# Block 3's first quarter of H by halves, and the order of sums and activations in Y of blocks 1 to 3

## The chip, the cores and the metric

The kernel runs on one core of one Trainium2 chip. The time is that of the device for one execution, in microseconds (us). Three runs of the kernel before gave 274.15, 274.19 and 273.52 us, so its median is 274.15 us.

The engines have short names in the profile: PE is TensorE (matrix products; PEld is its loading of weights), DVE is VectorE, ACT is ScalarE, POOL is GpSimd and SP is SyncE, which here only issues transfers.

## The reference

Linear attention with phi(x) = elu(x) + 1 over 8 batches of 8 heads, 576 rows and 64 columns, followed by two matrix products with a swish between them:

```python
q_p, k_p = phi(q), phi(k)                       # 8 x 8 x 576 x 64
kv  = einsum('bhsd,bhse->bhde', k_p, v)
z   = sum(k_p, axis=2)
num = einsum('bhsd,bhde->bhse', q_p, kv)
den = einsum('bhsd,bhd->bhs', q_p, z)[..., None] + 1e-06
x   = (num / den), as 4608 x 512
h   = x @ w_in                                  # 512 x 2048
g   = h / (1 + exp(-beta * h))
out = g @ w_out                                 # 2048 x 512
```

## The kernel before, in words

**Blocks and stages.** A block is one batch. Of its 576 rows 512 go through the two big products as a block; the 64 rows left over of all eight batches together make a last block, number 8. After a long start (block 0 and the attention of block 1) a loop runs over b = 1 to 8. Each turn has two stages: H (x times w_in, then swish into g, 16 tiles `ff` of 128 columns of w_in) and Y (g times w_out into the output). Beside these two stages of block b the attention of block b+1 (kv, numerators, transposes of x) runs in H, and phi of block b+2 runs in Y.

**The order is written by hand.** The program is scheduled manually: each engine executes its instructions in the order of the source. A step of the attention is hung onto a step of H or Y with `at(sh, n, f)` or `at(sy, n, f)`, and `run(side, n)` issues it there. So the numbers in the loop at the end of the file (lines 1031 to 1074) are the schedule.

**H in two forms.** `h_phase` makes all 16 tiles plainly: four matmuls of 512 columns into one PSUM bank, then one activation (`silu`). `h_fast` makes tiles 0 to 3 by halves instead: seven products of half size (`h_products`, four matmuls of 256 columns each, 28 in all against 16 of 512) of sums of w_in (`h_w_sums`, once) and of sums of x (`h_x_sums`, once per block: four subtractions on DVE into `h_xs`, which is the memory of `xs_sb`). Six DVE sums (`part0` to `part3`) put the products together, and `out` activates the results. Between the products stand plain tiles, so that DVE has time. Before the change blocks 1 to 3 use `h_phase`, blocks 4 to 8 `h_fast`; blocks 7 and 8 make two quarters by halves.

**Y** (`y_fast`) uses halves throughout: seven products of 16 matmuls of 256 columns, in the order pa, pd, pa, pc, pb, pd, pb, on four banks. DVE makes `gs` for it (`g_diff`, `g_sums`), u2 and u3 (lines 987 and 988) and the four quarters of the result. The second product into pb can start only when the sum at line 997 has read the first; the second into pd only when line 988 has read pd.

**PSUM.** Pool `hps` has four single banks that go round among the plain tiles, the first half product, two banks of the numerators, and Y. Pool `wps` has two pairs that go round among kv, the numerators (`numer_all`, two pairs) and the half products (`hc`, `hz`).

**Queues.** SyncE issues the transposes of phi of q (`q_trans_dma`, tile qTd) and of x (`trans` in `numer_all`, tile xT) and the stores of the output, in program order. GpSimd issues the loads: `next_loads(n)` first copies one element of qTd (`gate`), so that nothing is loaded for the next block before the transposes have landed, then issues v, q and k of block n+1, and casts v (`v_copy`). `tail_copy` saves the 64 rows left over, also on GpSimd.

Of the kernel before, what the change touches and what calls it, by code (L numbers as in the profile page):

```python
# [11 lines left out]
ACTF = mybir.ActivationFunctionType  # L12
# [4 lines left out]
def kernel(  # L17
# [39 lines left out]
    def banks(name, shape=None, dt=F32):  # L57
        return wps.tile(shape or [P, 2, 512], dt, tag="w", name=name)
# [95 lines left out]
    def table(func):  # L154
        nc.scalar.activation(act0, warm[:, 0:1], func)  # L155
# [57 lines left out]
    def kv_both(b):  # L213

        t = banks("kvp")
        for pr in range(2):
            for j in range(J):  # L220
                for il in range(2):
                    for a in range(2):
                        nc.tensor.matmul(  # L223
                            t[half(il), a, pr * EA : (pr + 1) * EA],
                            st[b, "k"][half(a), pr, j, il * D : (il + 1) * D],
                            vaug[b % 2][half(a), pr, j, il, 0:EA],
                            start=(j == 0), stop=(j == J - 1), skip_group_check=True,
                        )
        tv = t[:, :, 0 : 2 * EA].rearrange("p a (r e) -> p a r e", r=2)
        if b > 1:  # L230
            nc.vector.tensor_copy(kv_q[b % 2], tv)
            return
        st[b, "kv"] = kv_bd.rearrange("p a r h e -> p a r (h e)")
        for il in range(2):
            nc.vector.tensor_copy(kv_bd[half(il), :, :, il], tv[half(il)])
# [83 lines left out]
    def numer_all(b):  # L319

        h = [bank("nps"), bank("nps")]
        w = [banks("nps") for _ in range(2)]
        for v in (*range(7, 14), *range(7), *range(14, 18)):
            t, a = v // 4, v % 2
            for il in range(2):
                ps = h[il] if v // 7 == 1 else w[v // 14][:, il]  # L330
                for n in range(2):
                    pr, j = (v % 4 // 2, 2 * t + n) if v < 16 else (n, J - 1)
                    nc.tensor.matmul(
                        ps[half(n), v % 7 * EA : (v % 7 + 1) * EA],
                        st[b, "qTd"][half(il), a, pr * J + j, :],
                        kv_q[b % 2][half(il), a, pr, :],
                        start=True, stop=True, skip_group_check=True,
                    )

        def evac(ps, ils, v0, v1):  # L340

            m, i, u = len(range(*ils.indices(2))), v0 % 7, v1 - v0
            pv = ps[:, :, i * EA : (i + u) * EA].rearrange("p i (u e) -> p i u e", e=EA)
            den = work.tile([P, 2, 7], F32, tag="den", name="den")[:, :m, :u]
            rden = work.tile([P, 2, 7], F32, tag="rden", name="rden")[:, :m, :u]
            nc.vector.tensor_scalar(den, pv[:, :, :, D], 1e-6, None, ALU.add)
            nc.vector.reciprocal(rden, den)
            nc.vector.tensor_mul(  # L348
                xs_sb[:, ils, v0 * D : v1 * D].rearrange("p i (u d) -> p i u d", d=D),
                pv[:, :, :, 0:D], rden[:, :, :, None].to_broadcast([P, m, u, D]),  # L350
            )

        def trans(v0, v1):
            for il in range(2):
                nc.sync.dma_start_transpose(
                    out=xT[b % 2][:, il, v0 // 2 : v1 // 2],
                    in_=xs_sb[:, il, v0 * D : v1 * D],
                )

        for il in range(2):  # L360
            evac(h[il][:, None], slice(il, il + 1), 7, 14)
        evac(w[0], slice(0, 2), 0, 7)
        trans(0, 8)
        evac(w[1], slice(0, 2), 14, 18)
        trans(8, 18)
# [349 lines left out]
    def run(side, n):  # L715
        for f in side.get(n, ()):
            f()

    def at(side, n, *fs):
        side.setdefault(n, []).extend(fs)  # L720
# [69 lines left out]
            return xT_tail[:, :, 4 * t : 4 * t + 4, r]  # L790
        return xT[b % 2][:, :, 4 * t + r : 4 * t + 4 : 2]

    def h_x_sums(b, ks=range(4)):

        t = [h_xs[:, k] for k in range(4)]
        x = lambda r, t: h_x_plain(b, r, t)

        def like(a, c):
            return a.rearrange("p i (t n) -> p i t n", n=c.shape[-1])

        for k in ks:
            u, w = (
                (x(0, 1), x(0, 0)), (x(1, 1), t[0]), (x(1, 1), x(0, 1)), (x(1, 0), t[1])
            )[k]
            nc.vector.tensor_sub(like(t[k], u), u, like(w, u) if k % 2 else w)

    def h_products(b, fq):
# [55 lines left out]
    def h_fast(b, x, side):  # L863
        hps_of = {}

        def plain(ff):
            hps_of[ff] = bank("h_ps")
            h_mm(x, ff, hps_of[ff])

        def act(*ffs):  # L870
            for ff in ffs:
                silu(b, ff, hps_of[ff])

        def dual(*ffs):
            for ff in ffs:
                plain(ff)
                act(ff)

        if b < B - 1:
            dual(4)  # L880
            run(side, 0)
        p0, p1, p2, p3, out = h_products(b, 0)
        p0()

        dual(*((5,) if b < B - 1 else (4,)))
        p1()
        dual(*((6,) if b < B - 1 else (5,)))
        p2()
        dual(*((7,) if b < B - 1 else (6,)))
        p3()  # L890
        out(0)
        if b < B - 1:
            g_diff(b, slice(4, 8))
            dual(8, 9)
            out(1)
            run(side, 9)
            for ff in range(10, FC):
                dual(ff)
                if ff == 10:
                    g_diff(b, slice(0, 4))  # L900
                if ff in (11, 15):
                    g_sums(b, ff - 11, ff - 7)
            return
        run(side, 0)
        dual(7)
        out(1)
        p0, p1, p2, p3, out = h_products(b, 2)
        p0()
        dual(12)
        p1()  # L910
        dual(13)
        p2()
        g_diff(b, slice(0, 4))
        dual(14)
        p3()
        out(1, [0])
        g_diff(b, slice(4, 8))
        dual(15)
        out(1, [1])
        out(0)  # L920
        g_sums(b, 4, 8)
        g_sums(b, 0, 4)
# [108 lines left out]
    for b in range(1, B + 1):  # L1031
        n, m = b + 1, b + 2
        sh, sy = {}, {}
        if 2 <= b < 4 or b == B - 1:
            at(sh, 0, lambda: tail_copy(b))
        if n < B:
            at(sh, 0, lambda: next_loads(n))
            if b >= 4:
                at(sh, 0, lambda: tail_copy(b))
            at(sh, {1: 9, 2: 2}.get(b, 1 if b == 3 else 0), lambda: kv_both(n))  # L1040
            at(sh, {1: 11, 2: 5}.get(b, 4 if b == 3 else 9), lambda: numer_all(n))
        if b == 1:
            at(sh, 4, lambda: w_sum(2))
            at(sh, 9, lambda: w_sum(1))
            at(sy, 0, lambda: w_sum(3))
        if m < B:
            at(sy, 0, lambda: phi_tile(m, "q"), lambda: phi_tile(m, "k"))
            if b == 1:

                for pr in range(2):  # L1050
                    at(sy, 0, lambda pr=pr: v_copy(nc.scalar, m, pr))
                for pr in range(2):
                    at(sy, 0, lambda pr=pr: phi_exp(m, "q", pr, xin(m, "q", pr)))
                    at(sy, 3 + pr, lambda pr=pr: phi_relu(m, "q", pr, xin(m, "q", pr)))
                    at(sy, 3 + pr, lambda pr=pr: phi_min(m, "q", pr))
                at(sy, 4, lambda: q_trans_dma(m))
                at(sy, 5, lambda: phi_part(m, "k", 0))
                at(sy, 6, lambda: phi_part(m, "k", 1), lambda: table(ACTF.Silu))
            else:
                at(sy, 0, lambda: phi_part(m, "q", 0))  # L1060
                at(sy, 1, lambda: phi_part(m, "q", 1))
                at(sy, 1, lambda: q_trans_dma(m))
                at(sy, 3 if b < 4 else 4, lambda: phi_part(m, "k", 0))
                at(sy, 4, lambda: phi_part(m, "k", 1), lambda: table(ACTF.Silu))
        if b == 3:
            at(sh, 2, lambda: h_w_sums(0))
        if b == B - 2:
            at(sy, 4, lambda: h_w_sums(2))
        if 3 <= b < B:

            for i, step in enumerate((1, 6) if b < B - 2 else (0, 0)):
                at(sy, step, lambda i=i, n=n: h_x_sums(n, range(2 * i, 2 * i + 2)))
        (h_phase if b < 4 else h_fast)(b, xT[b % 2] if b < B else xT_tail, sh)
        y_fast(b, sy)


# [28 lines left out]
```

## Time and profile before

| | us |
|---|---|
| median of the three runs | 274.15 |
| the profiled execution's own time | 274.97 |
| its span, first to last instruction | 273.2 |
| PE busy | 265.4 (97%) |
| DVE busy | 204.1 (75%) |
| ACT busy | 168.8 (62%) |
| POOL busy | 43.6 (16%) |

The page gives for each engine the time in which it was busy. The "chain that ended last" is followed back from the last instruction, at each step to what released it; read in order of time it shows which engine carried the end. In that chain and in a timeline a line holds the start in us, the duration in us, the engine, the line of the source, the instruction's operands by their names in the program, and how many were merged (x16). In brackets stands how long the engine was idle before, and who released it. In the list of waits a line holds who waited, for whom, the total in us, how often, and the longest. PE's granted clock was 0.994 of full speed on average over the span.

### The profile page before, as it was taken

The numbers are of one execution on the slowest core, as the hardware profiler recorded it, in microseconds if no ns is written. First come the engines' busy times: TensorE is split into PE (matmuls) and PEld (weight loads), VectorE is DVE, ScalarE is ACT, GpSimd is POOL, SyncE is SP. The second block draws the span as 40 slices with busy tenths as digits, with TensorE's granted clock in tenths as the row PEclk, the third lists the DMA queues.
The fourth block names the chain that finished last, engine by engine and source line by source line (L and its number), as shares of the span: only waits on it lengthen the run. The fifth ranks groups of instructions, "written<-read, shape, count | busy, mean of one in ns | idle before, by whom it ended". The sixth has DMA issues, their size and how long they took to land.

```text
span 273.2 us, 6742 instructions
## 1 busy us (share of the span) xinstructions
PE 265.4 (97%) x2845; PEld 181.3 (66%) x2845; DVE 204.1 (75%) x392; ACT 168.8 (62%) x237; POOL 43.6 (16%) x64
## 2 busy tenths in 40 slices
PE   7899999999999999999999999999999999999994
PEld 2585455445865487548864886488657866886793
DVE  4871775899895778668868987898788767856862
ACT  3828896976777785588548854886473038405810
POOL 5922002034014020330033003300001000000000
PEclk9979999999999999999999999999999999999999
DMA  6999999656998996998589777995504050024013
GB/s 229 254 206 350 244 396 240 202 104 213 224 115 174 280 165 114 255 241 96 86 231 251 108 91 195 265 132 86 156 2 86 2 154 4 0 43 113 0 41 115
DMA packets 48958, 42.78 MB, mean 157 GB/s; under 512 B 30352, under 2 KB 40736, under 8 KB 48928
## 3 DMA queue, kind: packets, MB, share of 16 engines
q0 software_dynamic: 13040, 23.40, 36.8%
q1 hardware_dynamic: 35568, 18.75, 34.5%
q8 instruction: 22, 0.36, 0.5%
q10 hardware_dynamic: 320, 0.20, 0.3%
q14 instruction: 8, 0.07, 0.1%
HBM read 36.71 MB, written 9.44 MB: 169 GB/s over the span
## 4 chain that ended last, share of the span: by engine, by line
PE 79%; DVE 10%; DMA 6%; ACT 2%; issue 1%; SPq 0%; DVEq 0%
PE h_ps L402 30%; PE yd L964 9%; PE ya L964 9%; PE yb L964 8%; PE hc L820 4%; PE yc L964 4%; PE y_ps L417 4%; DMA xT<-xs_sb 4%; PE hz L820 3%; DMA stage<-in_q_dram 2%; PE kvp L223 2%; ACT g L856 1%; PE yb L936 1%; DVE r L169 1%; DVE phi_k L175 1%; DVE xs_sb L348 1%
## 5 line engine op out<-in xcount | busy, mean ns | idle before, releaser
L410 ACT ACTIVATE g<-h_ps,beta_c 128x512 bf16<-128x512 f32 x116 | 77.0, 688 | 58.7 <-PE h_ps L402 58.7
L402 PE MATMUL h_ps<-xT,w_in 128*128 128x512 bf16 (+1 forms) x480 | 100.0, 358 | 0.7 <-ACT g L410 0.5
L402 PEld LDWEIGHTS <-w_in 128*128 128x128 bf16 x512 | 46.9, 98 | 44.8 <-issue 0.9
L964 PEld LDWEIGHTS <-stage 128*128 128x128 bf16 x480 | 46.9, 98 | 5.8 <-issue 0.3
L964 PEld LDWEIGHTS <-g 128*128 128x128 bf16 x384 | 37.5, 98 | 6.0
L964 PE MATMUL ya<-w_out,g 128*128 128x256 bf16 x256 | 30.6, 273 | 0.0
L241 POOL CAST vaug<-vf 128x1152 bf16<-128x1152 f32 x11 | 12.8, 1190 | 43.0 <-DMA vf<-in_v_dram 15.4
L348 DVE TENSOR_TENSOR xs_sb<-nps,rden 128x448 bf16<-128x448 f32 (+2 forms) x24 | 18.2, 758 | 0.8
L162 ACT ACTIVATE e<-xk 128x1152 bf16<-128x1152 bf16 (+1 forms) x15 | 16.7, 1160 | 3.1 <-DMA xk<-in_k_dram 3.1
L162 ACT ACTIVATE e<-xq 128x1152 bf16<-128x1152 bf16 x14 | 15.6, 1159 | 2.4 <-DMA xq<-in_q_dram 2.0
L728 DVE TENSOR_TENSOR stage<-g 128x1024 bf16<-128x1024 bf16 x16 | 12.8, 798 | 5.6 <-ACT g L410 5.6
L155 ACT ACT_TABLE_LOAD x12 | 15.4, 1283 | 0.2
L964 PE MATMUL yd<-ws,stage 128*128 128x256 bf16 x128 | 15.3, 273 | 0.0
L964 PE MATMUL yc<-ws,stage 128*128 128x256 bf16 x128 | 15.3, 273 | 0.0
L964 PE MATMUL yd<-ws,g 128*128 128x256 bf16 x128 | 15.3, 273 | 0.0
L417 PE MATMUL y_ps<-w_out,g 128*128 128x512 bf16 x64 | 15.1, 379 | 0.0
L175 DVE TENSOR_TENSOR phi_q<-e,r 128x1152 bf16<-128x1152 bf16 x16 | 12.1, 758 | 3.2 <-ACT e L162 2.0
L175 DVE TENSOR_TENSOR phi_k<-e,r 128x1152 bf16<-128x1152 bf16 x16 | 12.8, 802 | 1.4
L964 PE MATMUL yb<-ws,stage 128*128 128x256 bf16 x112 | 13.4, 273 | 0.0
L964 PE MATMUL yb<-w_out,stage 128*128 128x256 bf16 x112 | 13.4, 272 | 0.0
L856 ACT ACTIVATE g<-hc,beta_c 128x512 bf16<-128x512 f32 x14 | 8.8, 682 | 6.8 <-DVE hc L849 6.8
L724 DVE TENSOR_TENSOR stage<-g 128x1024 bf16<-128x1024 bf16 x16 | 10.9, 682 | 1.9 <-ACT g L410 1.9
(135 smaller groups left out, 345.0 us busy)
## 6 DMA issues: line engine op xcount, KB each, us to landing
vf<-in_v_dram POOLq DMA_DIRECT2D x7, 1152.0 KB, 9.5
out_dram<-y SPq DMA_DIRECT2D x29, 256.0 KB, 4.3
xq<-in_q_dram POOLq DMA_DIRECT2D x7, 576.0 KB, 12.4
xk<-in_k_dram POOLq DMA_DIRECT2D x7, 576.0 KB, 15.1
w_in<-in_moe_w_in_dram POOLq DMA_DIRECT2D x4, 512.0 KB, 11.7
g<-in_moe_w_out_dram POOLq DMA_DIRECT2D x2, 1024.0 KB, 17.5
stage<-in_moe_w_out_dram POOLq DMA_DIRECT2D x2, 1024.0 KB, 21.4
stage<-in_q_dram SPq DMA_DIRECT2D x2, 576.0 KB, 4.6
```

Of the source, the lines that this page charges most:

```text
L155: nc.scalar.activation(act0, warm[:, 0:1], func)
L162: nc.scalar.activation(e, x, ACTF.Exp)
L175: nc.vector.tensor_tensor(st[b, a][:, pr].rearrange("p j (h d) -> p j h d", h=2), st[b, a, pr, "e"].rearrange("p h j d -> p j h d"), st[b, ...
L241: eng.tensor_copy(dst, src)
L348: nc.vector.tensor_mul(xs_sb[:, ils, v0 * D : v1 * D].rearrange("p i (u d) -> p i u d", d=D), pv[:, :, :, 0:D], rden[:, :, :, None].to_bro ...
L402: nc.tensor.matmul(hp[:, c0:c1].rearrange("p (t n) -> p t n", n=n), w_in_sb[ff // 4][:, kc, (ff % 4) * P : (ff % 4 + 1) * P], xm, start=(k ...
L410: nc.scalar.activation(g_sb[b % 2][:, ff, :], hp, ACTF.Silu, scale=beta_c[:, ff : ff + 1])
L417: nc.tensor.matmul(yp[:, c0:c1], g_sb[b % 2][:, ff, t * P : (t + 1) * P], w_out_sb[i][:, c, c0:c1], start=(ff == 0), stop=(ff == FC - 1), ...
L728: nc.vector.tensor_add(gs[0][:, c], g[:, c, HM:512], g[:, c2, HM:512])
L820: nc.tensor.matmul(o, lhs[:, i, a * P : (a + 1) * P], m, start=(first and a == 0 and i == 0), stop=True, skip_group_check=True,)
L856: nc.scalar.activation(g_sb[b % 2][:, ff].rearrange("p (t n) -> p t n", t=2), src, ACTF.Silu, scale=beta_c[:, ff : ff + 1],)
L964: nc.tensor.matmul(ps[:, p * HM : (p + 1) * HM], lhs(c, p), rhs(c), start=(first and p == 0 and c == 0), stop=True, skip_group_check=True,)
```

## The change

Five things change, and the step numbers that follow from them.

1. `h_phase` runs for blocks 1 and 2 only; block 3 now uses `h_fast`. `h_w_sums(0)` moves from H of block 3 (step 2) to H of block 2 (step 9).
2. In `h_fast` of blocks 3 to 6 the plain tile 5 comes before the first half product, and the plain tiles between the products are one number higher. The numerators move from step 9 to step 10. In block 3 kv moves from step 1 to 0 and the numerators from step 4 to 10; in block 2 kv from 2 to 3 and the numerators from 5 to 6.
3. The four sums of x stand together behind Y (step 6 of Y of blocks 2 to 5). Before, two stood at step 1 of Y and two at step 6, for blocks 3 to 5. In Y of blocks 6 and 7 they stay at step 0.
4. In `numer_all` the two pairs of banks change places.
5. In Y of block 1 the operations of phi are spread anew over the steps: maximum of q's second half at step 5, minima of q at 4 and 5, transposes of q at 5 instead of 4, and k's parts at 5 and 6. In Y of blocks 2 and 3 the first half of phi of k moves from step 3 to 4. On GpSimd the tail copy of block 3 moves behind the loads.

```diff
-        w = [banks("nps") for _ in range(2)]
+        w = [banks("nps") for _ in range(2)][::-1]
...
-    def h_x_sums(b, ks=range(4)):
+    def h_x_sums(b):
...
+        n = 6 if b < B - 1 else 4
         if b < B - 1:
             dual(4)
             run(side, 0)
+            dual(5)
         p0, p1, p2, p3, out = h_products(b, 0)
         p0()
-        dual(*((5,) if b < B - 1 else (4,)))
+        dual(n)
         p1()
-        dual(*((6,) if b < B - 1 else (5,)))
+        dual(n + 1)
         p2()
-        dual(*((7,) if b < B - 1 else (6,)))
+        dual(n + 2)
         p3()
         out(0)
         if b < B - 1:
             g_diff(b, slice(4, 8))
-            dual(8, 9)
+            dual(9, 10)
             out(1)
-            run(side, 9)
-            for ff in range(10, FC):
+            run(side, 10)
+            for ff in range(11, FC):
                 dual(ff)
-                if ff == 10:
+                if ff == 11:
                     g_diff(b, slice(0, 4))
                 if ff in (11, 15):
                     g_sums(b, ff - 11, ff - 7)
...
-        if 2 <= b < 4 or b == B - 1:
+        if b == 2 or b == B - 1:
             at(sh, 0, lambda: tail_copy(b))
         if n < B:
             at(sh, 0, lambda: next_loads(n))
-            if b >= 4:
+            if b > 2:
                 at(sh, 0, lambda: tail_copy(b))
-            at(sh, {1: 9, 2: 2}.get(b, 1 if b == 3 else 0), lambda: kv_both(n))
-            at(sh, {1: 11, 2: 5}.get(b, 4 if b == 3 else 9), lambda: numer_all(n))
+            at(sh, {1: 9, 2: 3}.get(b, 0), lambda: kv_both(n))
+            at(sh, {1: 11, 2: 6}.get(b, 10), lambda: numer_all(n))
...
-                    at(sy, 3 + pr, lambda pr=pr: phi_relu(m, "q", pr, xin(m, "q", pr)))
-                    at(sy, 3 + pr, lambda pr=pr: phi_min(m, "q", pr))
-                at(sy, 4, lambda: q_trans_dma(m))
-                at(sy, 5, lambda: phi_part(m, "k", 0))
-                at(sy, 6, lambda: phi_part(m, "k", 1), lambda: table(ACTF.Silu))
+                    at(sy, 3 + 2 * pr, lambda pr=pr: phi_relu(m, "q", pr, xin(m, "q", pr)))
+                    at(sy, 4 + pr, lambda pr=pr: phi_min(m, "q", pr))
+                at(sy, 5, lambda: q_trans_dma(m))
+                for pr in range(2):
+                    at(sy, 5, lambda pr=pr: phi_exp(m, "k", pr, xin(m, "k", pr)))
+                    at(sy, 5 + pr, lambda pr=pr: phi_relu(m, "k", pr, xin(m, "k", pr)))
+                    at(sy, 6, lambda pr=pr: phi_min(m, "k", pr))
+                at(sy, 6, lambda: table(ACTF.Silu))
...
-                at(sy, 3 if b < 4 else 4, lambda: phi_part(m, "k", 0))
+                at(sy, 4, lambda: phi_part(m, "k", 0))
...
-        if b == 3:
-            at(sh, 2, lambda: h_w_sums(0))
+        if b == 2:
+            at(sh, 9, lambda: h_w_sums(0))
...
-        if 3 <= b < B:
-            for i, step in enumerate((1, 6) if b < B - 2 else (0, 0)):
-                at(sy, step, lambda i=i, n=n: h_x_sums(n, range(2 * i, 2 * i + 2)))
-        (h_phase if b < 4 else h_fast)(b, xT[b % 2] if b < B else xT_tail, sh)
+        if 2 <= b < B:
+            at(sy, 6 if b < B - 2 else 0, lambda: h_x_sums(n))
+        (h_phase if b < 3 else h_fast)(b, xT[b % 2] if b < B else xT_tail, sh)
```

More of the change, by code (lines that the diff above doesn't have):

```diff
@@ L799, in like @@
             return a.rearrange("p i (t n) -> p i t n", n=c.shape[-1])
[L801 to L804, printed above, removed]
+        for k, (u, w) in enumerate((
+            (x(0, 1), x(0, 0)), (x(1, 1), t[0]), (x(1, 1), x(0, 1)), (x(1, 0), t[1])
+        )):
             nc.vector.tensor_sub(like(t[k], u), u, like(w, u) if k % 2 else w)
```

## The prediction

> **What bounds the kernel now.** I read the page's busy shares first, then the chain that ended last, then the timelines of VectorE, GpSimd and SyncE around the places that the diff touches.
>
> ```profile
> PE 265.4 (97%) x2845; PEld 181.3 (66%) x2845; DVE 204.1 (75%) x392; ACT 168.8 (62%) x237; POOL 43.6 (16%) x64
> PE 79%; DVE 10%; DMA 6%; ACT 2%; issue 1%; SPq 0%; DVEq 0%
> ```
>
> TensorE is busy 97% of the span, and from block 2 on the chain is almost only PE. So a change is worth the PE time it takes out plus the PE waits it removes or makes. Nothing else counts until PE waits for it. The chain in order of time (start, duration, what), from the second product of Y of block 2 that ends late to the middle of H of block 4:
>
> ```profile
> 104.55 1.75 PE yd L964 x16
> 106.30 1.89 PE yb L964 x16
> 108.19 1.73 PE h_ps L402 x8
> 109.91 0.86 PE kvp L223 x72
> 110.77 2.70 PE h_ps L402 x12
> 113.47 0.76 PE nps L333 x72
> 114.23 9.60 PE h_ps L402 x44
> 123.83 1.75 PE ya L964 x16
> ...
> 136.06 0.86 PE h_ps L402 x4
> 136.93 0.74 PE kvp L223 x72
> ...
> 143.45 0.71 DVE hc L849
> 144.19 1.26 ACT g L856 x2
> 145.45 0.59 ACT g L410
> 146.08 5.34 PE h_ps L402 x24
> 151.42 1.75 PE ya L964 x16
> ```
>
> Differences of these starts give the stages: H of block 3, all plain, takes 123.83 - 108.19 = 15.64 us; H of block 4, with a quarter by halves, 151.42 - 136.06 = 15.36 (blocks 5 and 6: 15.38 and 15.37). Y of block 2 takes 12.37, Y of block 3 and later 12.23. The four lines before 146.08 are the price of the halves: the last sum of the products (L849), two activations of them and one of a plain tile must end before PE gets its next bank. PE's starts put that wait at 0.25 us (from the numerators' last matmul to the next 0.37 us; 0.125 in blocks 2 and 3).
>
> VectorE in Y of block 2, and the cast on GpSimd with the VectorE sum beside it in H of block 3:
>
> ```profile
> 103.57 0.69 DVE L988 TENSOR_TENSOR u<-yd,u 128x512 f32<-128x512 f32 x1
> 104.17 0.59 DVE L169 TENSOR_SCALAR r<-xk 128x1152 bf16<-128x1152 bf16 x1
> 104.87 0.76 DVE L175 TENSOR_TENSOR phi_k<-e,r 128x1152 bf16<-128x1152 bf16 x1
> 105.55 0.68 DVE L997 TENSOR_TENSOR y<-yb,u 128x512 f32<-128x512 f32 x1
> ```
> ```profile
> 119.96 2.24 POOL L241 CAST vaug<-vf 128x1152 bf16<-128x1152 f32 x2 [8.42 <-DMA vf<-in_v_dram]
> ```
> ```profile
> 121.14 1.60 DVE L728 TENSOR_TENSOR stage<-g 128x1024 bf16<-128x1024 bf16 x1 [2.04 <-ACT g L410]
> ```
>
> L997 frees the bank of the last product of Y. It stands behind phi of k, ends at 106.23, and that product, due at 106.14, starts 0.146 us late: the 0.14 by which Y of block 2 is long. And a bf16 sum that takes 0.69 us elsewhere took 1.60 while GpSimd cast.
>
> **Part 1: block 3 by halves.** Removed: 16 matmuls of 512 columns, 4 of which are 0.86 us in the chain, 3.46 us. Added: 28 of 256 columns, 4 of which are 0.435 (0.44, and 0.87 for 8), 3.05 us. Gain 0.41. The bank wait comes along: order and banks behind the last product are those of blocks 4 to 6, only the tile numbers are one higher, so +0.25. The kv product took 0.86 in block 3 and 0.74 elsewhere, by one pause of 0.105 in the middle that no other block has; I take it as gone, -0.11. Sum -0.27, which is 15.64 against the 15.36 to 15.38 of the blocks that do this already. If the pause stays, -0.16.
>
> The Trainium skill speaks against such halving ("TensorE: Matmul & The Clock Gate", Back-to-back issue gap): in a real stream it gives some 131 ns for a matmul of 512 columns and some 81 for 128. By that, as an estimate, 16 x 131 = 2.1 us would give way to at least 28 x 81 = 2.3, a loss of 0.2 or more. The chain's 216 and 109 ns per matmul decide against it.
>
> VectorE gains work in block 3: six sums of 0.69 (4.1 us) in H, four x sums of 0.42 behind Y of block 2 (1.6), and h_w_sums moves to step 9 of block 2 (1.5). Cover: h_w_sums falls between g_diff and g_sums, where VectorE idles 1.28 us at 91.8 to 93.1; the numerators' evacuation, a tile later, eats 0.86 of that, so g_sums(0:4) ends some 1 us later, while the next sum waits for ACT until 96.58 anyway. The x sums run 109.0 to 110.6, the kv copy to 111.0; the first product's result is there at about 111.0. Without that cover each would hold the products by its own length.
>
> **Part 2: numerators a tile later, blocks 3 to 6.** PE does the same work in another order: 0. In VectorE everything from the evacuation on moves 0.86 us. Covers, from block 4's rows: the second sum L729 ends 154.05 + 0.86 = 154.9, needed half a product into yc (156.66 in the chain); g_diff(0:4) ends 150.7 + 0.86 = 151.5, needed at 153.2; phi of q ends 0.86 later, but the two x sums that stood there (0.87 us) are gone, and VectorE idled 0.42 before u2. The four transposes of x go out 0.86 later, with nothing else in SyncE's queue then; in block 6 they land at 210.8 + 0.9, the four x sums end at 213.4, and u2 starts at 213.7. So 0, with 0.3 us left at the narrowest place. In block 3 the numerators move by six tiles: its four transposes start at about 122.0 instead of 117.5, and with the 8.4 to 10 us that they took under load they land by 132, before H of block 4 at 135.5. In block 2 kv and numerators move one tile: x lands at 103.9 + 0.9, needed at 107.9: 0. The x sums all behind Y: four end 1.6 us after L1008, before the copy of the first product, which itself comes 0.86 later: 0.
>
> **Part 3: order of two banks.** Numerators 0 to 6 take the pair that the second product frees, 14 to 17 that of the first. The burst of 72 took 0.76 with and without halves, so it did not wait: 0.
>
> **Part 4: Y of blocks 1 and 2.** Block 2: L997 starts when its product ends, 104.6 instead of 105.55; the 0.146 goes. Next on the path is kv of block 4, now at step 0: phi of k ends at 107.8, PE gets there at 108.8. Block 1: L997 stands before phi's minimum, so the same wait (0.16 before the last product, 77.6) goes, but H of block 2 waits for x's transposes (landing about 79.8 and 80.3) whatever Y does:
>
> ```profile
> PEld L402 <- DMA xT<-xs_sb: 0.3, 1, 0.3
> ```
>
> So 0 from block 1. The step to watch is the transpose of q for block 3, moved to step 5. SyncE before, and the gate on GpSimd that starts all loads of the next block:
>
> ```profile
> 79.20 3.54 SPq L273 DMA_TRANSPOSE qTd<-phi_q  x2
> ```
> ```profile
> 85.56 0.53 POOL L1025 COPY gate<-qTd 128x1 bf16<-128x1 bf16 x1 [4.42 <-DMA qTd<-phi_q]
> ```
>
> It now queues behind phi of q, whose minimum ends at 79.7 (79.05 before), and behind two stores of y2 (0.6 each, from 78.5): issue about 79.85, 0.65 later. How much longer the stores ahead of it in the same queue hold it no row shows. Call the whole delay d: at least 0.65, at most, by the far row of x's transposes under load (10.7 us to landing against 4.2 for q's), 7. I take 0.95: no loads run at that time (the last landed at 78.7), and the stores themselves took 1.2 longer behind transposes than later ones alone (4.4 against 3.2), of which I give a quarter. What d meets: numerators of block 3, at PE 87.1, bear d = 1.6. The loads for block 4 move by d, so does the cast, which holds a sum of block 2 until it ends (98.15 + d); phi of q then ends at 102.1 + d and u2, due at 102.84, slips by d - 0.81; the next product into its bank has 0.07 to spare. So Y of block 2 loses d - 0.88: 0.07 for my d.
>
> In block 3 the cast ends at 122.2 + d, near the end of the evacuation (122.8), so g_diff slips by some 0.2, with over 1 us left before Y needs it. The Trainium skill ("SBUF — State Buffer", Who interferes with whom) says that an operation with two SBUF inputs and a GpSimd read exclude each other for a whole instruction, which would fit the 1.60; if a full cast of 1.15 hit there, it would still be under that slack. On GpSimd, block 3's tail copy now stands behind the loads and casts; only the last stage reads it: 0.
>
> **Sum.** -0.27 - 0.146 + 0.07 = -0.35 us. On the profiled execution's own time (274.97, a span of 273.2 and 1.8 around it) that is 274.62; it ran 0.82 over the median of the runs, so on the median of 274.15 it is 273.8. A measurement here tells 0.3%, 0.82 us, from no change.
>
> **Rivals.** (a) *Late q, slower.* If the transposes start only when the stores have landed (stores took 3.6 to 4.4 us, so 83 instead of about 80.5), d is about 3.1 and Y of block 2 with H before it loses 3.1 - 0.88 = 2.2: 274.15 - 0.42 + 2.2 = 275.9. It decides from d = 2.1 on (0.42 + 0.82 + 0.88). For it: x's transposes under load take 10 us. Against: stores and transposes overlap at 82.85, where a store issued before the transposes had landed was only 1.2 late.
> (b) *Nothing comes of it.* The kv pause returns (0.11), d is 1.2 (0.32): -0.42 + 0.11 + 0.32 is no change, 274.1. For it: every term is a tenth of a microsecond. Against: three blocks run the same H at 15.36 to 15.38.
> (c) *Clearly faster.* The bank wait of 0.25 goes in all four blocks with the new order, 0.98 in all: 272.8. For it: numerators take two of four banks, and their place moves. Against: the tiles around them move along.
>
> **How the numbers follow.** Forecast 0.58, (b) 0.20, (a) 0.14, (c) 0.08. The forecast's own range is 273.4 to 274.2. Forecast and (b) are within 0.3%, save some 0.08 that the runs' own spread (273.52 to 274.19) puts over a bound, half on each side: faster 0.12, same 0.70, slower 0.18. The range reaches up to d = 2, 274.15 - 0.42 + 1.12, about 274.9, and down to 273.1, a third of the way to (c); two thirds of (a) and (c) stay out, 0.15.
>
> **What would show it.** H of block 3 at 15.36 to 15.4 with the chain through L849 and L856 as in block 4; Y of block 2 at 12.23 to 12.3; H and Y of blocks 4 to 6 unchanged within 0.05. The gate of block 2 at 86.2 to 86.6. Wrong if Y of block 2 is over 13, if the numerators of block 2 wait for qTd, if a yc or yd product waits for VectorE in blocks 3 to 6, or if H of block 2 starts later than 80.1.

## The result

The changed kernel takes 275.28 us, the median of 21 runs (274.50 to 276.99); the kernel before takes 274.15 us in 21 runs of the same session (273.43 to 274.85). The ratio is 1.0047, with a 95% interval of 1.0033 to 1.0061: slower by about 1.1 to 1.3 us, where 273.8 us was forecast. It is rival (a), in which the transposes of q come late.

The page of the changed kernel hides it well. PE's share of the span falls by one point. In the summary of the chain PE falls from 79% to 66% and DMA rises from 6% to 17%, but 8 points of the 17 are a load of v that the chain now meets in the long start (19.03 to 40.64 us), which the change leaves alone:

```profile
PE 263.3 (96%) x2852; PEld 181.7 (66%) x2857; DVE 208.4 (76%) x402; ACT 167.8 (61%) x237; POOL 43.9 (16%) x64
PE 66%; DMA 17%; DVE 10%; ACT 3%; issue 1%; SPq 1%; POOL 0%; DVEq 0%; POOLq 0%
```

The chain in order of time (start, duration, what) shows the place. These are its lines from the end of x's transposes in Y of block 1 to the half products of block 3:

```profile
70.62 8.81 DMA xT<-xs_sb
...
79.97 1.67 SPq L273
...
81.68 6.08 DMA qTd<-phi_q
...
87.80 0.83 PE nps L333 x72
88.63 7.88 PE h_ps L402 x36
96.50 1.75 PE ya L965 x16
...
108.73 0.86 PE h_ps L402 x4
109.59 0.78 PE kvp L223 x72
110.38 0.97 PE h_ps L402 x4
111.35 0.44 PE hz L819 x4
...
117.03 0.71 DVE hc L848
...
117.76 1.27 ACT g L855 x2
119.03 0.59 ACT g L410
...
119.66 4.48 PE h_ps L402 x20
124.14 1.75 PE ya L965 x16
```

The numerators of block 3 (nps at 87.80) hang on the transposes of q, qTd, which are now on the path. Before, the path ran through PE here without a break:

```profile
83.62 2.69 PE h_ps L402 x12
86.32 0.76 PE nps L333 x72
```

PE's timeline of the changed kernel gives the wait in brackets, and SyncE's shows what stands ahead of the transposes now:

```profile
87.80 0.83 PE L333 MATMUL nps<-kv_q,qTd 64*64 64x65 bf16 x72 [1.48 <-DMA qTd<-phi_q]
```
```profile
78.04 1.31 SPq L1005 DMA_DIRECT2D out_dram<-y  x2
79.52 4.08 SPq L273 DMA_TRANSPOSE qTd<-phi_q  x2
83.71 2.04 SPq L1011 DMA_DIRECT2D out_dram<-y  x2
```

The prediction had named this wait as a sign of being wrong. PE's starts give the stages from H of block 2 on, each from its first matmul to that of the next (the differences are taken before rounding). Spans can't be compared directly: H of block 1 began at 50.6 to 53.3 us in the profiles of this study, after a start that the change leaves alone, and the profiled execution of the kernel before (274.97 us) was one of its longer runs.

| stage | before, us | changed, us | difference |
|---|---|---|---|
| H of block 2 | 15.73 | 17.28 | +1.55 |
| Y of block 2 | 12.37 | 12.23 | -0.14 |
| H of block 3 | 15.64 | 15.41 | -0.24 |
| H of blocks 4, 5, 6 | 15.36, 15.38, 15.38 | 15.40, 15.39, 15.37 | +0.05 in all |
| from H of block 2 to the last matmul | 189.25 | 190.45 | +1.20 |

The sum of the stages, 1.20 us, is close to the difference of the medians, 1.13. So everything that the change was worth (-0.38) is there, and one wait of 1.55 us is paid on top: by PE's starts, 1.64 us of pause before the numerators against 0.09 before.

### The profile page after: what moved, and what is told of

Same layout as the page of the kernel before. It is cut to its first block, busy times and chain, and to the rows that moved or that the text cites. A ratio compares the mean times of both kernels' runs of the same rounds, so it can differ in the third digit from the quotient of the medians.

```text
span 273.5 us, 6774 instructions
## 1 busy us (share of the span) xinstructions
PE 263.3 (96%) x2852; PEld 181.7 (66%) x2857; DVE 208.4 (76%) x402; ACT 167.8 (61%) x237; POOL 43.9 (16%) x64
## 4 chain that ended last, share of the span: by engine, by line
PE 66%; DMA 17%; DVE 10%; ACT 3%; issue 1%; SPq 1%; POOL 0%; DVEq 0%; POOLq 0%
PE h_ps L402 21%; DMA vf<-in_v_dram 10%; PE ya L965 9%; PE yd L965 9%; PE yb L965 8%; PE hc L819 5%; PE yc L965 4%; PE hz L819 4%; DMA xT<-xs_sb 3%; DMA qTd<-phi_q 2%; ACT g L855 2%; PE kvp L223 1%; DMA stage<-in_q_dram 1%; PE yb L937 1%; DVE xs_sb L348 1%
## 5 line engine op out<-in xcount | busy, mean ns | idle before, releaser
L410 ACT ACTIVATE g<-h_ps,beta_c 128x512 bf16<-128x512 f32 x112 | 73.9, 690 | 60.3 <-PE h_ps L402 60.3
L402 PE MATMUL h_ps<-xT,w_in 128*128 128x512 bf16 (+1 forms) x464 | 97.7, 357 | 0.9 <-ACT g L410 0.7
L402 PEld LDWEIGHTS <-w_in 128*128 128x128 bf16 x496 | 45.1, 98 | 41.8 <-issue 1.1
L855 ACT ACTIVATE g<-hc,beta_c 128x512 bf16<-128x512 f32 x16 | 10.1, 683 | 8.1 <-DVE hc L848 8.1
L175 DVE TENSOR_TENSOR phi_k<-e,r 128x1152 bf16<-128x1152 bf16 x16 | 12.8, 803 | 1.3
L175 DVE TENSOR_TENSOR phi_q<-e,r 128x1152 bf16<-128x1152 bf16 x16 | 12.1, 758 | 1.9 <-ACT e L162 0.8
L724 DVE TENSOR_TENSOR stage<-g 128x1024 bf16<-128x1024 bf16 x16 | 10.9, 682 | 2.0 <-ACT g L410 2.0
L819 PEld LDWEIGHTS <-w_in 128*128 128x128 bf16 x96 | 9.4, 98 | 4.5
```

The source lines that it names most:

```text
L175: nc.vector.tensor_tensor(st[b, a][:, pr].rearrange("p j (h d) -> p j h d", h=2), st[b, a, pr, "e"].rearrange("p h j d -> p j h d"), st[b, ...
L402: nc.tensor.matmul(hp[:, c0:c1].rearrange("p (t n) -> p t n", n=n), w_in_sb[ff // 4][:, kc, (ff % 4) * P : (ff % 4 + 1) * P], xm, start=(k ...
L410: nc.scalar.activation(g_sb[b % 2][:, ff, :], hp, ACTF.Silu, scale=beta_c[:, ff : ff + 1])
L724: nc.vector.tensor_sub(gs[2][:, c], g[:, c, 0:HM], g[:, c, HM:512])
L819: nc.tensor.matmul(o, lhs[:, i, a * P : (a + 1) * P], m, start=(first and a == 0 and i == 0), stop=True, skip_group_check=True,)
L855: nc.scalar.activation(g_sb[b % 2][:, ff].rearrange("p (t n) -> p t n", t=2), src, ACTF.Silu, scale=beta_c[:, ff : ff + 1],)
```

## The experiments

Times are medians; each run's ratio is to runs of the kernel before on the same chip. "Run 3" is the changed program of experiment 3. Unless said otherwise an edit is to the changed kernel. "Landing" of the transposes is that of the second one, and "the minimum of phi of q" is the last operation of phi (L175), after which the transposes can start.

**1. Stores of y2 behind the transposes.** Only the place of the two stores moves.

```diff
+        if b == 1:
+            run(side, 5)
         for i in range(2) if b < B else ():
             nc.sync.dma_start(out=rows(b, slice(4 + i, 4 + i + 3, 2)), in_=y2[half(i)])
-        run(side, 5)
+        if b != 1:
+            run(side, 5)
```

> The changed kernel with one thing moved: in Y of block 1 the two stores of y2 are issued behind the two transposes of q (and behind phi's operations of that step) instead of ahead of them. VectorE's order stays that of the change. Theory (the stores ahead in SyncE's queue hold the transposes up on the DMA side by some 2 us): the second transpose lands about 2 us earlier against the start of H of block 2, at about +6.6 us, the numerators at +7.2 no longer wait 1.55 us, and the time falls from 275.28 to about 273.7. Rival 1 (the later minimum of phi of q alone makes them late): at least 1 us of the wait stays, time 274.8 to 275.3. Rival 2 (the loss lies in block 3 by halves or later): no change, 275.3.

Measured: 274.16 us, ratio 1.0009 (0.9991 to 1.0027). The wait at the numerators is gone (H of block 2: 15.52). The gate on GpSimd, which starts as soon as the second transpose has landed, stands at 86.02, 6.9 us after the start of H of block 2; in the changed kernel it stood at 87.87, 8.8 after it. But the time stops some 0.45 short of the 273.7 that was expected, and Y of block 2 lost about that much: it took 12.62 instead of 12.23. Its PE line names the sum u3 (L989), which frees the bank of yd:

```profile
103.77 1.47 PE L965 MATMUL yd<-ws,g 128*128 128x256 bf16 x12 [0.23 <-DVE u L989]
```

VectorE before it, in the same run: two sums of g held to 1.5 us (0.69 elsewhere), while GpSimd cast v (95.64 to 98.81), and then phi of q waiting for its exponential, for which ScalarE waited 1.68 us on the load of q.

```profile
96.29 1.52 DVE L729 TENSOR_TENSOR stage<-stage,g 128x1024 bf16<-128x1024 bf16 x1
97.84 1.51 DVE L730 TENSOR_TENSOR stage<-g,stage 128x1024 bf16<-128x1024 bf16 x1
99.28 0.45 DVE L169 TENSOR_SCALAR r<-xq 128x1152 bf16<-128x1152 bf16 x1
100.39 0.76 DVE L175 TENSOR_TENSOR phi_q<-e,r 128x1152 bf16<-128x1152 bf16 x1 [0.67 <-ACT e L162]
```

Against the start of H of block 2 the transposes landed 1.26 us later than before (6.78 against 5.52). The prediction's formula for this price, d - 0.88, gives 0.38; measured 0.39. So close a match is in part luck: in the profile of run 9, whose edit does not touch this stage, Y of block 2 took 12.52 instead of 12.37.

**2. The same stores from GpSimd's queue.**

```diff
-            nc.sync.dma_start(out=rows(b, slice(4 + i, 4 + i + 3, 2)), in_=y2[half(i)])
+            (nc.gpsimd if b == 1 else nc.sync).dma_start(
+                out=rows(b, slice(4 + i, 4 + i + 3, 2)), in_=y2[half(i)]
+            )
```

> The changed kernel, the two stores of y2 in Y of block 1 at the same place of the program but issued from GpSimd's queue instead of SyncE's. It tells whether the same queue is what holds the transposes, or any store in flight with them. Same queue: the numerators' wait of 1.55 us goes, 273.7. Stores in flight on the shared DMA engines: 0.5 to 1.5 us of it stay, 274.2 to 275.3. Rival 2 (block 3): 275.3.

Measured: 275.44 us, ratio 1.0049 (1.0035 to 1.0063). The wait stays at nearly its full size (1.38 us in PE's brackets against 1.48), though SyncE's queue has nothing ahead of the transposes and starts to issue them 0.15 us after the minimum of phi of q:

```profile
79.02 1.25 POOL L1005 DMA_DIRECT2D out_dram<-y  x2 [14.41 <-DVE y L1001]
...
88.08 0.19 POOL L1028 COPY gate<-qTd 128x1 bf16<-128x1 bf16 x1 [7.29 <-DMA qTd<-phi_q]
```
```profile
80.10 4.51 SPq L273 DMA_TRANSPOSE qTd<-phi_q  x2
```

So it is not the order in one queue. Stores that are in flight when the transposes start hold them up, from either of the two queues. The Trainium skill ("DMA: Bandwidth & Descriptors", Issuing engines are not separate DMA queues) states what fits this: transfers of all issuing engines end up on the same 16 DMA engines and interleave, and issuing from another engine saves only the sequencer's time. The run agrees: the stores' packets from GpSimd's queue run until 83.4 us, those of the transposes beside them from 81.7 on, and the wait is about as long from either queue.

**3. Y of block 1 as before.** The steps of phi in Y of block 1 are put back; the rest of the change stays.

> The changed kernel with the steps of phi in Y of block 1 as they were before; all else as changed. Theory and rival 1 both expect the numerators' wait in block 2 to go and the time to be 275.28 - 1.55 = 273.7; the wait of 0.16 us in Y of block 1 comes back, hidden by the wait for the transposes of x at the start of H of block 2. Rival 2 (block 3 by halves or the later stages lose): about 275.3, still slower than before.

Measured: 273.75 us, ratio 0.9986 (0.9973 to 1.0000), as expected. The numerators don't wait, Y of block 2 takes 12.23, H of block 3 15.40. This is the change without the part that lost: faster by 0.3 to 0.4 us, as the sum forecast, though the interval just reaches no change.

**4. Y of block 1 alone.** The kernel before, with only the new steps of phi in Y of block 1.

> The kernel before with the new steps of phi in Y of block 1 alone. Theory: here the numerators of block 3 stand one tile earlier in H of block 2, so they wait 1.55 + 0.86 = 2.4 us for the transposes of q, and the time is about 274.15 + 2.4 = 276.5; at least 276 if the landing is a little earlier. Rival 2: 274.1, no change.

Measured: 275.62 us, ratio 1.0063 (1.0039 to 1.0087). This part alone makes the kernel slower by 1.6 us. The expected 276.5 (at least 276) did not come. The wait was smaller than the 2.4 expected: in the profile, which is of the fastest run, 1.3, since the landing came 7.4 us after the minimum of phi of q, against 8.5 in the changed kernel. The six runs took 274.58 to 277.12 us; that the holding differs from run to run would explain this spread, but only one of them has a profile.

**5. No stores of y2 in block 1.**

```diff
-        for i in range(2) if b < B else ():
+        for i in range(2) if 1 < b < B else ():
```

> The changed kernel with the two stores of y2 in block 1 left out (a quarter of the output of one block is not written); VectorE's and PE's order as changed. It parts the two causes of the late transposes. Theory: the stores in flight hold them by 2 us, so the second lands 6.3 us after the minimum of phi of q instead of 8.5, some 6.5 us after the start of H of block 2, the numerators at +7.2 do not wait, and the time is 275.28 - 1.55 + 0.1 = 273.8. Rival (the later minimum is enough): a wait of 1 us or more stays, 274.8 or more.

This kernel leaves a quarter of one block's output unwritten. Measured: 273.97 us, ratio 0.9985 (0.9963 to 1.0007). The minimum of phi of q is as late as in the changed kernel (0.3 and 0.2 us after the start of H of block 2), the numerators don't wait, Y of block 2 takes 12.23. With runs 1 and 2 this parts the causes. The time from the end of that minimum to the landing of the second transpose was

| kernel | stores of y2 | us |
|---|---|---|
| before; run 3 | behind the transposes | 6.4; 6.2 |
| run 1 | behind the transposes | 6.4 |
| run 5 | none | 6.2 |
| changed | ahead, SyncE | 8.5 |
| run 2 | ahead, GpSimd | 8.0 |
| run 4 | ahead, SyncE | 7.4 |
| run 6 | ahead, SyncE | 8.4 |

Stores ahead cost 1.0 to 2.1 us against the kernel before. The later minimum, by itself, costs another 1.0 against the start of H of block 2 (0.87 ahead of it before, 0.17 after it in the changed kernel), which the numerators' later step just bears.

**6. Numerators of block 3 two tiles later** (step 8 instead of 6 in H of block 2).

> The changed kernel with the numerators of block 3 two tiles later in H of block 2 (step 8). The transposes of q stay late, but PE comes to the numerators at +8.9 us, after their landing at about +8.7. Theory (the loss is the wait at the numerators; the loads for block 4, started by the same landing, cost little): the wait goes, Y of block 2 takes 12.2 to 12.5, time 273.8 to 274.1. Rival (what is late at the numerators is paid again through the loads): Y of block 2 takes 13 or more, 274.7 or more.

Measured: 274.72 us, ratio 1.0019 (0.9999 to 1.0039). This is nearer to the rival: the wait at the numerators goes, but Y of block 2 takes 12.91. About half of the loss is paid elsewhere: from H of block 2 on the profile is 0.86 us longer than run 3's, that of the changed kernel 1.68. The casts now fall on two sums of g, which stand later as well, and u3 comes late for yd:

```profile
96.06 1.59 DVE L729 TENSOR_TENSOR stage<-stage,g 128x1024 bf16<-128x1024 bf16 x1
97.69 1.52 DVE L730 TENSOR_TENSOR stage<-g,stage 128x1024 bf16<-128x1024 bf16 x1
```
```profile
95.97 2.70 POOL L241 CAST vaug<-vf 128x1152 bf16<-128x1152 f32 x2 [4.51 <-PE h_ps L402]
```
```profile
105.09 1.14 PE L965 MATMUL yd<-ws,g 128*128 128x256 bf16 x9 [0.53 <-DVE u L989]
```

Taking the wait away where it shows is not the same as taking the lateness away.

**7. Block 3 plain again**, on the kernel of run 3: `h_phase` for blocks 1 to 3, kv at step 1 and numerators at step 4 in block 3.

> The changed kernel with Y of block 1 as before, and block 3 plain again (kv at step 1 and numerators at step 4 as before); the new steps of blocks 4 to 6, of block 2 and of Y of blocks 2 and 3 stay. It takes the halves' share out of the gain of 0.31 to 0.40 us. Theory: H of block 3 takes 15.6 instead of 15.40, Y of block 2 stays at 12.23, time 273.75 + 0.24 = 274.0. Rival (the halves in block 3 gain nothing in the time, all comes from Y of block 2): 273.75.

Measured: 273.74 us, ratio 0.9987 (0.9977 to 0.9996), against 0.9986 with the halves. That is the rival's time; the times don't tell the halves' share. The profile has H of block 3 at 15.52 plain against 15.40 by halves, 0.12 us; the 15.64 of the kernel before held the pause of 0.105 in kv, which two profiles of the plain block lack (this run and run 9) and two others have (run 4 and run 11).

**8. The last sum of the half products first**, on the kernel of run 3, blocks 3 to 6.

```diff
-            product(z, w(1, 1), t[3], False)
+            if b >= B - 1:
+                product(z, w(1, 1), t[3], False)
             product(cw[:, 0], w(0, 1), h_x_plain(b, 1, 0), False)
             product(cw[:, 1], s[3], h_x_plain(b, 1, 1), False)
+            if b < B - 1:
+                product(z, w(1, 1), t[3], False)
+                nc.vector.tensor_add(cw[:, 1], cw[:, 1], h_u[0])
             nc.vector.tensor_add(c2[:, 0], z, h_u[0])
-            nc.vector.tensor_add(cw[:, 1], cw[:, 1], h_u[0])
+            if b >= B - 1:
+                nc.vector.tensor_add(cw[:, 1], cw[:, 1], h_u[0])
```

> The changed kernel with Y of block 1 as before (273.75), and in the last part of the half products of blocks 3 to 6 another order: the two products into the pair hc first, the one into hz last, and the sum that finishes hc ahead of the other. Nothing is added. Theory (PE's wait of 0.25 us per block behind the numerators is the chain last sum, two activations, one plain activation): the sum starts one product, 0.44 us, earlier, which is more than 0.25, so the wait goes in blocks 3 to 6 and H takes 15.15 there instead of 15.40; time 273.75 - 0.98 = 272.8. Rival (the wait is for the bank behind the numerators' own evacuation or for a late plain tile): H stays at 15.40, time 273.7.

Measured: 272.85 us, ratio 0.9963 (0.9951 to 0.9976), the best of the study, with an interval clear of no change. The chain goes through PE alone here, also behind the numerators:

```profile
115.48 0.44 PE hz L819 x4
115.91 1.73 PE h_ps L402 x8
117.64 0.76 PE nps L333 x72
118.40 4.42 PE h_ps L402 x20
```

H of blocks 3 to 6 takes 15.24, 15.24, 15.21 and 15.22. So the bank wait of 0.25 is gone in each, but 0.08 of it comes back: the first product into hc now starts 0.08 late, behind the sum that still reads that pair. The gain against run 3 is 4 x 0.16 = 0.64, not 0.98; the ratios, 0.9986 and 0.9963, say the same. That the time hit the expected 272.8 is luck: run 3 was timed on another chip, where the kernel before took 274.06 us and not 273.96.

**9. That order alone, on the kernel before** (blocks 4 to 6).

> The kernel before with that order of the last part alone (blocks 4 to 6). Theory: three waits of 0.25 us go, 274.15 - 0.74 = 273.4, H of blocks 4 to 6 at 15.11 to 15.13 instead of 15.36 to 15.38. Rival: 274.1. It also measures this order by itself, without block 3 by halves.

Measured: 273.47 us, ratio 0.9991 (0.9982 to 0.9999), a gain of some 0.25 us by the ratio where 0.74 was expected. H of blocks 4 and 6 takes 15.20 and 15.23, of block 5 15.42: there the sum that reads hc ran late and the product waited 0.29 for it. The gain is there in two of the three blocks.

**10. Both orders:** run 8, and in Y of block 1 the first sum of Y ahead of phi's minima, with transposes and stores in the order of before (`phi_min` of q at step 4 for both halves).

> As the first kernel here, and in Y of block 1 the first sum into the output's second half moved ahead of phi's two minima of q, while the second minimum and the transposes stay ahead of the next sum and of the stores. So the bank wait of 0.16 us in Y of block 1 goes without making the transposes of q later: their second landing stays within 0.3 us of that of the first kernel here. Theory: 272.8 - 0.16 = 272.6, unless x's transposes take the wait's place at the start of H of block 2 (then 272.8). Rival (any new order in Y of block 1 makes the transposes late): the numerators of block 2 wait again, 273.5 or more.

Measured: 272.94 us, ratio 0.9960 (0.9948 to 0.9973), the same as run 8. The transposes land in time, but x's transposes take the place of the bank wait at the start of H of block 2, as the second branch of the expectation has it. Sums ahead of phi do no harm as long as the transposes stay ahead of the stores, and in block 1 they bring nothing.

**11. The new step of phi of k in Y of blocks 2 and 3 alone**, on the kernel before.

> The kernel before with one thing of the change: in Y of blocks 2 and 3 the first half of phi of k at step 4 instead of 3. Theory: Y of block 2 takes 12.23 instead of 12.37 and nothing else moves, 274.15 - 0.14 = 274.0. Rival: the wait moves to kv of block 4 in H of block 3, which then takes 15.66 or more, and the time stays at 274.1.

Measured: 274.19 us, ratio 0.9993 (0.9973 to 1.0014). Y of block 2 takes 12.23 as expected, and H of block 3 stays at 15.63. The time can't tell 0.14 us.

**12. The two pairs of banks in their old order**, on the kernel of run 3.

> The changed kernel with Y of block 1 as before, and the two pairs of banks of the numerators in their old order. Theory: the exchange of pairs was worth nothing, since the burst of 72 never waited; in blocks 3 to 6 H takes 15.40 as with the exchange and the burst 0.76 us. Rival: the burst waits for the activations of hc, H takes 15.5 or more in these blocks.

Measured, in a single run of 273.77 us: H of blocks 3 to 6 at 15.40, 15.40, 15.38 and 15.38, as with the exchange. It is worth nothing here.

## Why the prediction was wrong

**The step that failed** is in part 4, where the delay d of q's transposes is sized: "I take 0.95", with a quarter of 1.2 us given to the stores ahead. Against the start of H of block 2 the landing moved from 5.52 to 8.69 us, so d was 3.17: 1.04 from the later minimum (forecast 0.65) and 2.1 from the stores (forecast 0.3). Rival (a) had put d at 3.1, and the late q that it describes is what happened; the mistake was to weigh it at 0.14. The row that I held against it, a store that lost only 1.2 us behind transposes, is about the opposite order: it shows what a store loses, and not what a transpose loses. The pair of transposes, issued in 3.54 us before, took 4.08 with stores ahead (the first of the two 2.11 instead of 1.29).

Rival (a)'s mechanism, transposes that start only when the stores have landed, explains part of the 2.1 us. By the trace's packet records the first packet of the transposes (256 bytes each, where a store's have 2048) ran 1.2 us after the start of their issue in the kernel before and in runs 1, 3 and 5, and 2.1 us after it in the changed kernel and in runs 4 and 6 (1.6 in run 2). In the changed kernel that is at 81.59, behind the landing of the first store (81.41). This is 0.9 us. Most of the rest lies at the other end: from the last packet to the landing it took 2.0 us in the changed kernel (85.72 to 87.75) and 0.6 before. What made that end late no run shows.

**Rival (a)'s price** was 2.2 us in H and Y of block 2 together; measured 1.55, all at the numerators, which is d - 1.6 as the prediction's bound for them says. The rest, up to d - 0.88, did not come, because the loads behind the same landing ran faster: in the changed kernel v landed 5.8 us after its issue against 9.1 before, most likely since the stores that used to run beside it were done. The formula for Y of block 2 takes the loads to be as slow as before. In run 1, where the numerators don't wait and v took 9.0, it holds; in run 6, where they don't wait either but v took 6.6, it gives 2.3 and Y lost 0.68.

**Part 1** was forecast at -0.27 and is -0.24 between the two profiles, with the bank wait of 0.25 in block 3 as forecast (the lines at 117.03 to 119.66). Half of this was the pause in kv, which is not a property of the plain block; without it the halves are worth 0.12 (run 7). The prediction had named that case (-0.16). The 216 and 109 ns per matmul hold in block 3 too: 0.86 us for four plain matmuls and 0.44 for four of half size. So the 131 ns for 512 columns that the Trainium skill gives ("TensorE: Matmul & The Clock Gate", Back-to-back issue gap) do not fit here.

**Part 2** was forecast at 0, and H of blocks 4 to 6 and Y of blocks 3 to 6 differ by less than 0.05 from before. **Part 3**, 0, is what run 12 shows. **Part 4 for block 2**, -0.146, is 12.37 to 12.23, in the changed kernel and alone (run 11). For block 1 the bank wait went and brought nothing, as forecast, because x's transposes set the start of H. That reason is not general: in the profiles of runs 1 to 3 PE did not wait for them there.

**Rival (c)** did not happen: the bank wait stayed, for which the tiles around the numerators, which moved along, are the likely reason. Run 8 shows what does remove it. **Rival (b)** had the pause come back in block 3 by halves. It did not (kv took 0.78 us there); but since the plain block can do without it too, its 0.11 us was no gain of the halves.

## What to carry to other kernels

When a step is moved past a transfer, price the transfers that will then be in flight with its own, from all queues, and not only its place in one queue; nobody waited for the stores that run 1 moved out of the way. Before such a move, list who starts on its landing: here PE and a gate of all loads, so that hiding the first waiter only hands the lateness to the second. And where a wait is a chain of last sum, activations and bank, look at whether the sum can start earlier; it was worth 0.16 us per block here, and the halving of block 3's quarter 0.12.

## What the runs showed of the hardware

The pair of DMA transposes of q for block 3 took 6.0 to 6.4 us from the data being ready to the second landing in all profiles without stores ahead, and 7.4 to 8.5 with two stores of 256 KB each issued about 1 us ahead of them, from the same queue or from another one. SyncE itself was held too: the first of the two transposes, which it issued in 1.29 us before, took 2.11 with stores in flight. I had expected a delay of some 0.3 us.

A pause of 0.105 us in the middle of 72 small matmuls of kv stood in some profiles of the same stage and not in others. A difference of that size between two single profiles is no term for a sum.
